# Threshold attention with an RWKV feed-forward: the first five batches taken in two halves of their queries, and new step durations in the planner

## The chip, the cores and the metric

The kernel runs on one core of one Trainium2 chip. The metric is the device time of one launch in microseconds (us); smaller is better. Times are medians of several runs. Besides these there is one profiled execution, whose trace all rows below come from. Engines are named as the profile names them: PE is the matrix engine (its weight loads are PEld), DVE the vector engine, ACT the scalar engine, POOL GpSimd, SP the engine whose queue issues every DMA of this kernel.

## What is computed

Attention of 8 batches, 8 heads, 576 positions and head dimension 64, in which every probability whose score is more than tau under its row's largest is dropped; its output feeds an RWKV channel mix (called FFN here) of width 512 and inner width 1024.

```python
scores = scale * np.matmul(q, k.transpose(0, 1, 3, 2))
thresh = np.max(scores, axis=-1, keepdims=True) - tau
scores = np.where(scores >= thresh, scores, -1000000000.0)
attn = np.exp(scores - np.max(scores, axis=-1, keepdims=True))
attn = attn / (np.sum(attn, axis=-1, keepdims=True) + 1e-09)
x = np.matmul(attn, v)            # then heads side by side: (8, 576, 512)

x_prev = x shifted by one position, zero first
xk = mu_k * x + (1.0 - mu_k) * x_prev
xr = mu_r * x + (1.0 - mu_r) * x_prev
k = np.maximum(xk @ w_k, 0.0)     # 512 -> 1024
v = k * k @ w_v                   # 1024 -> 512
r = 1.0 / (1.0 + np.exp(-(xr @ w_r)))
out = r * v
```

## The kernel before

**The work.** Heads are taken in pairs, four pairs (hp) to a batch. A *job* is one pair of one batch; a *unit* is one block of 128 queries of both heads (kind P, blocks 0 to 3) or the last 64 queries of both heads together (kind T). A P unit makes two score tiles of 128x576, a T unit one; so a batch has 36 score tiles, and the 8 batches have 288. The counter `n` numbers these tiles in the order in which jobs are listed.

**A job's operands** (`operands`): one DMA of queries and keys into `raw` (two buffers), a scaling on ACT (L412), the high part `hi` on ACT (L430, one buffer), the rest `lo` on POOL in two instructions (L436, one buffer), eight DMAs (L455) that stack both into `st1` and `st2` (three buffers each, two of which one job holds), and a DMA of `v` (two buffers). The first two jobs are `plain` and skip `hi`, `lo` and `st`.

**A unit** (`softmax`, `turn_pair`, `turn_last`): scores on PE (L517 from `st` for P units, L492 from `hi` and `lo` directly for T units), row maximum on DVE (L551), threshold and exponential on ACT (L559, L567), mask and sum on DVE (L575), the reciprocal on DVE (L585, L586), the division on POOL (L600), transposes on PE (L624), and their eviction (L642 on ACT, L644 on DVE). With more than `EARLY` tiles behind it, the second of a unit's two big evictions goes to DVE; until then both go to ACT.

**Attention's product** (`attend`, L704) is made for two groups of a job: group 0 from query blocks 0 and 1, group 1 from 2 and 3; the T unit goes with group 0, or with the second part where the job is halved. While its key is under `EARLY` it is cut in five PE steps.

**The FFN** (`ffn_chunk`) works on 256 positions: mixing on POOL, DVE and ACT (L797 to L827), 96 matmuls with w_k (L849), squares on ACT and POOL (L857 to L872), 24 matmuls with w_r (L891), a sigmoid, 48 matmuls with w_v (L913), and the products to the output (L919, DMAs L929). There are 16 chunks from groups and 2 more from the T queries of four batches each, 18 in all. A group's chunk can start when all four pairs of the batch have that group.

**Halving.** Batch 0 is already listed in two parts, which is the only place where the order of units differs:

```python
halved = {0: ([0, 1], [2, "T", 3])}
```

All four pairs run blocks 0 and 1 first, then all four run blocks 2, T and 3. Each part of each pair is a job of its own, so its operands are loaded twice. The other batches run T, 0, 1, 2, 3 of one pair after another.

**What sets the order.** Nothing is scheduled at run time: `Plan.order` places all steps in one list, by expected start on their engine (`s.occ`, `s.lat`, DMA times), then by key. Matmuls and transposes of attention have keys that are 1000 lower than the FFN's, so the FFN fills what they leave on PE. `LATE` puts 0.3 us on attention's PE steps that start after `FROM`; `SOFT` makes the FFN's and the weights' steps on DVE and ACT look later than they are. On the chip each engine runs its own list strictly in order, and so does SP's queue.

**Weights.** 20 pieces of the three weight matrices are taken from 64-bit words by `weight` during the first part of the order: one ACT step, four DVE steps (L355, L369, L376, L386), an ACT and a POOL step each.

Of the kernel before, what the change touches and what calls it, by code (L numbers as in the profile page):

```python
# [48 lines left out]
class Plan:  # L49

    HOP, LATE, FROM = 0.05, 0.3, 150.0
    SOFT = {"DVE": 0.3, "ACT": 0.3}

    def __init__(self):
        self.steps = []
# [54 lines left out]
    def order(self, loose=()):  # L112
# [23 lines left out]
        pipe = 0.0  # L136
# [2 lines left out]

        def when(s):  # L140
            t = s.ready
            more = {}
            for b in s.allocs:
                if id(b) in placed:
                    continue
                m = more.get(b.tag, 0)
                more[b.tag] = m + 1
                if b.tag not in loose and self.tags[b.tag][turn[b.tag] + m] is not b:
                    return None
                h = sorted(freed[id(o)] if o else -1.0 for o in held[b.tag] if not (o and left[id(o)]))  # L150
                if len(h) <= m:
                    return None
                t = max(t, h[m] + self.HOP)
            return t

        total = len(steps)
        while len(out) < total:
            best = None
            for e, cand in open_.items():
                f = free[e]  # L160
                pick = None
                for i in cand:
                    s = steps[i]
                    t = when(s)
                    if t is None:
                        continue
                    t = max(t, f)
# [7 lines left out]
            _, e, i, t = best  # L175
            s = steps[i]
# [2 lines left out]
            free[e] = t + s.occ  # L179
            if e == "DMA":  # L180
                pipe = max(pipe, t) + s.kb / 260.0
                s.end = max(t + 2.2, pipe + 1.5)
            else:
                s.end = t + s.lat
            for b in s.allocs:
                if id(b) not in placed:
                    placed.add(id(b))
                    h = held[b.tag]
# [26 lines left out]
def tile_threshold_attention_then_rwkv_ffn(  # L215
# [12 lines left out]
    V, A, G, PE, SY = nc.vector, nc.scalar, nc.gpsimd, nc.tensor, nc.sync  # L228
# [26 lines left out]
    plan = Plan()  # L255
    add = plan.add
    DQ = 0.55
    W0, W1, W2, W3, AVK = 3.0, 3.5, 50.0, 2.0, 4.5
    PREP, PB, VB, COLD, EARLY = 6, 2, 2, 24, 16
    EV = ("ACT", 0.49), ("DVE", 0.6)  # L260
    KMAX, KEXP, KMASK = 0.0, 0.0, 0.5

# [6 lines left out]
    def fixed(name, shape, dtype=F32):  # L269
# [13 lines left out]
        writes=[(small, 0)],  # L283
        key=-100,
# [5 lines left out]
        reads=[(small, 0)],  # L290
# [32 lines left out]
    def weight(j, name, w, c, f, key, wait):  # L323
# [8 lines left out]
        def t():  # L332
# [18 lines left out]
        )  # L351
        add(
            "DVE",
            0.46,
            lambda: V.tensor_scalar(t(), t(), W_MIN, W_MAX, op0=ALU.max, op1=ALU.min),  # L355
            writes=box,
            key=key,
# [5 lines left out]
        def word(y):  # L363
# [1 line left out]

        add(
            "DVE",
            0.46,
            lambda: V.tensor_scalar(u(), u(), 0x07FFFFFF, 3, op0=ALU.bitwise_and, op1=ALU.logical_shift_left),  # L369
            writes=box,  # L370
            key=key,
        )
        add(
            "DVE",
            0.7,
            lambda: V.scalar_tensor_tensor(  # L376
                u(), word(1), 0xC0000000, u(), op0=ALU.bitwise_and, op1=ALU.bitwise_or
            ),
# [3 lines left out]
        )  # L382
        add(
            "DVE",
            0.7,
            lambda: V.scalar_tensor_tensor(  # L386
                u(), word(0), 29, u(), op0=ALU.logical_shift_right, op1=ALU.bitwise_or
            ),
# [74 lines left out]
    def scores(unit, ss, key):  # L463
# [32 lines left out]
        if unit["kind"] == "T" or job["plain"]:  # L496

            last = unit["kind"] == "T"

            def both():  # L500
                for z in range(2):
                    for h in range(2):
                        hr = slice(h * D, (h + 1) * D)
                        o = ss[1].get()[hr, z, 0:HS] if last else ss[h].get()[:, z, 0:HS]
                        q = slice(SM, S) if last else slice(c * P, (c + 1) * P)
                        PE.matmul(o, raw.get()[hr, q], raw.get()[hr, keys(h, z)], start=True, stop=True)

            occ = 1.2 if last or key > COLD else 2.3
            add("PE", occ, both, reads=[raw], writes=list(ss.values()), key=key - 1000, lat=occ + 0.25)
            return  # L510
        for y in range(2):
# [15 lines left out]
    def softmax(unit):  # L527
# [56 lines left out]
        def invert():  # L584
# [2 lines left out]

        add(
            "DVE",
            0.29,  # L590
            invert,
            reads=[(sm, (2, y)) for y in ys],
            writes=[(sm, (3, y)) for y in ys],
# [24 lines left out]
    def transposes(p, y, at, key, to):  # L618
# [6 lines left out]
                    pt.get()[:, c, :], p.get().rearrange("p y s -> p (y s)")[:, o : o + P], ident.get()  # L625
                )

        occ = 0.109 * len(at)
        add(
            "PE",  # L630
            occ,
# [122 lines left out]
    def ffn_chunk(kind, b0, g, key):  # L754
# [35 lines left out]
        for hc in range(0, NCT, 2):  # L790
# [9 lines left out]
            for j in range(2):  # L800
# [11 lines left out]
                                op1=ALU.add,  # L812
                            )

                add("DVE", 0.8 if nseg == 1 else 1.57, scale, reads=[diff, mu_sb, *sr], writes=[d], key=key)
                add(
                    "ACT",
                    0.52,
# [116 lines left out]
        plan.soft = False  # L935


    halved = {0: ([0, 1], [2, "T", 3])}
    PLAIN = 2
    jobs = []  # L940
    n = 0
# [94 lines left out]
```

## Time and profile before

| | |
|---|---|
| median of 3 runs | 1117.92 us (1116.38 to 1119.11) |
| the profiled execution's own time | 1118.3 us |
| span of the profiled execution, first to last instruction | 1116.5 us |
| mean granted PE clock in it | 0.972 of full speed |
| busy: PE / DVE / ACT / POOL | 93% / 70% / 66% / 52% |

Between the span and the execution's own time lie 1.8 us. Busy shares are means over stages of different kinds: the first batch with the weights, seven batches in which attention and FFN are mixed, and an end in which only FFN chunks are left.

### The profile page before, as it was taken

The page shows a single profiled execution, that of the slowest core. Times are in us where ns is not written, and L with a number is a line of the kernel's source. Part 1 is how long each engine was busy: PE and PEld are TensorE (multiplying, and loading weights), DVE is VectorE, ACT ScalarE, POOL GpSimd, SP SyncE. Part 2 cuts the span into 40 slices and gives each one's busy share as a digit, 9 for nine tenths or more (in the row PEclk, how much of TensorE's full clock was granted, in tenths as well). Part 3 has the DMA queues.
Part 4 walks back from the last instruction along what each step waited for, and adds up shares of the span by engine and source line. Part 5 has one row for each costly group of instructions (what it writes and reads, how often), then busy time and mean ns, then how long its engine had stood idle before and what let it go on. Part 6 is the DMA issues. An engine that isn't in the chain of part 4 may idle for free.

```text
span 1116.5 us, 19374 instructions
## 1 busy us (share of the span) xinstructions
PE 1037.2 (93%) x6832; PEld 852.4 (76%) x6832; DVE 785.5 (70%) x1712; ACT 736.0 (66%) x1543; POOL 578.6 (52%) x582
## 2 busy tenths in 40 slices
PE   5767878898999999999999999999999989999998
PEld 3446656776877878778789878886788869788887
DVE  6889988877878878877887749765888488422220
ACT  5676776675885876776878666775687557344443
POOL 3575765544564555554656535554465544444441
PEclk8777989999999999999999999999999999999999
DMA  6997365544444435444455314441544141000000
GB/s 218 241 269 226 92 162 132 127 113 119 103 102 119 118 84 139 116 110 111 111 130 137 89 43 121 101 108 37 128 115 118 34 92 39 19 20 20 20 19 19
DMA packets 40639, 117.78 MB, mean 105 GB/s; under 512 B 6752, under 2 KB 6752, under 8 KB 40544
## 3 DMA queue, kind: packets, MB, share of 16 engines
q1 hardware_dynamic: 40544, 116.55, 41.0%
q8 instruction: 55, 0.90, 0.3%
q14 instruction: 40, 0.33, 0.1%
HBM read 44.70 MB, written 9.44 MB: 48 GB/s over the span
## 4 chain that ended last, share of the span: by engine, by line
PE 73%; DVE 13%; ACT 6%; DMA 4%; issue 3%; POOL 1%; SPq 0%; POOLq 0%; ACTq 0%
PE w L913 16%; PE w L849 15%; PE w L704 11%; PE w L624 11%; PE s L517 10%; PE w L891 8%; DVE p L575 4%; PE s L492 2%; ACT p L567 2%; DVE sm L551 2%; DMA raw<-in_qk 1%; DVE sm L585 1%; DMA st<-lo 1%; DMA wk<-in_w_k 1%; DVE mk L806 1%
## 5 line engine op out<-in xcount | busy, mean ns | idle before, releaser
L600 POOL TENSOR_SCALAR p<-p,sm 128x576 f32<-128x576 f32 x288 | 225.5, 792 | 268.9 <-DVE sm L586 227.1
L575 DVE SCALAR_TENSOR_TENSOR p<-s,sm,p 128x576 f32<-128x576 f32 x288 | 232.4, 813 | 58.3 <-ACT p L567 57.1
L551 DVE TENSOR_REDUCE sm<-s 128x1 f32<-128x576 f32 x288 | 210.8, 751 | 40.6 <-PE s L517 27.9
L849 PE MATMUL w<-xk,wk 128*128 128x256 f32 x1728 | 231.0, 284 | 0.0
L913 PE MATMUL w<-wv,k 128*128 128x512 f32 x864 | 221.1, 397 | 0.0
L849 PEld LDWEIGHTS w<-xk,wk 128*128 128x128 f32 x1728 | 216.5, 190 | 1.2 <-issue 0.5
L624 PE MATMUL w<-ident,p 128*128 128x128 f32 x1312 | 197.0, 285 | 19.8 <-POOL p L600 14.8
L567 ACT ACTIVATE p<-s,sm 128x576 f32<-128x576 f32 x288 | 210.2, 730 | 0.6
L624 PEld LDWEIGHTS w<-ident,p 128*128 128x128 f32 x1312 | 156.5, 145 | 58.3 <-POOL p L600 32.1
L913 PEld LDWEIGHTS w<-wv,k 128*128 128x128 f32 x864 | 156.4, 189 | 28.7 <-issue 0.8
L642 ACT ACTIVATE pm<-w 128x512 f32<-128x512 f32 x169 | 99.7, 593 | 98.2 <-PE w L624 96.8
L704 PE MATMUL w<-pm,v 128*64 128x256 f32 (+1 forms) x1024 | 148.4, 425 | 5.2 <-DVE pm L644 4.3
L806 DVE SCALAR_TENSOR_TENSOR mk<-m,mu_sb,xT 128x256 f32<-128x256 f32 x128 | 88.6, 732 | 83.5 <-POOL xk L827 83.4
L517 PE MATMUL s<-st 128*128 128x288 f32 x496 | 119.1, 322 | 27.3 <-DVE p L575 11.7
L827 POOL TENSOR_TENSOR xk<-mk,xk 128x512 fp32r<-128x512 f32 x72 | 94.0, 1306 | 92.8 <-ACT xk L819 87.2
L559 ACT ACTIVATE sm<-sm,small 128x1 f32<-128x1 f32 x288 | 83.5, 290 | 83.4 <-DVE sm L551 80.3
L872 POOL TENSOR_TENSOR k<-r,k 128x512 fp32r<-128x512 f32 x72 | 93.8, 1304 | 81.8 <-ACT k L862 81.5
L704 PEld LDWEIGHTS w<-pm,v 128*64 128x64 f32 x1024 | 71.6, 141 | 64.1 <-issue 10.3
L517 PEld LDWEIGHTS s<-st 128*128 128x128 f32 x496 | 79.7, 193 | 51.4 <-issue 29.0
L436 POOL TENSOR_TENSOR lo<-raw,hi 128x576 fp32r<-128x576 f32 x68 | 102.1, 1518 | 31.2 <-ACT hi L430 23.7
L517 PE MATMUL s<-st,st 128*128 128x288 f32 x496 | 110.6, 305 | 0.0
L891 PE MATMUL w<-wr,xk 128*128 128x512 f32 x432 | 109.4, 396 | 0.4 <-ACT pm L642 0.4
(62 smaller groups left out, 1142.9 us busy)
## 6 DMA issues: line engine op xcount, KB each, us to landing
raw<-in_qk SPq DMA_DIRECT2D x36, 608.0 KB, 5.1
st<-hi SPq DMA_DIRECT2D x68, 304.0 KB, 3.2
st<-lo SPq DMA_DIRECT2D x68, 304.0 KB, 4.3
v<-in_v SPq DMA_DIRECT2D x36, 320.0 KB, 4.2
st<-hi SPq DMA_DIRECT2D x68, 144.0 KB, 3.4
st<-lo SPq DMA_DIRECT2D x68, 144.0 KB, 3.9
out<-sg SPq DMA_DIRECT2D x32, 256.0 KB, 2.0
wk<-in_w_k SPq DMA_DIRECT2D x8, 512.0 KB, 7.5
```

Source lines behind the costliest of these rows:

```text
L436: lambda cs=cs: G.tensor_tensor(lo.get()[:, cs], raw.get()[:, cs], hi.get()[:, cs].bitcast(F32), op=ALU.subtract),
L517: PE.matmul(ss[y].get()[:, z, 0:HS], l.get()[:, c * P : (c + 1) * P], r.get()[:, keys(y, z)], start=(j == 0), stop=(j == 1),)
L551: lambda sv=sv, col=col: V.tensor_reduce(col(0), sv(), axis=AX.XY, op=ALU.max, negate=True),
L567: lambda sv=sv, pv=pv, col=col: A.activation(pv(), sv(), AF.Exp, bias=col(0)),
L575: lambda sv=sv, pv=pv, col=col: V.scalar_tensor_tensor(pv(), sv(), col(1), pv(), op0=ALU.is_ge, op1=ALU.mult, accum_out=col(2)),
L600: lambda y=y: G.tensor_scalar(p.get()[:, y], p.get()[:, y], sm.get()[:, 3, y : y + 1], 0.0, op0=ALU.mult, op1=ALU.add),
L624: PE.transpose(pt.get()[:, c, :], p.get().rearrange("p y s -> p (y s)")[:, o : o + P], ident.get())
L704: PE.matmul(o.get()[hs, 0:n], vt.get()[:, c, hs], pt[:, 0:n], start=(c == 0), stop=(c == 4))
L806: V.scalar_tensor_tensor(d.get()[:, y, o : o + n], diff.get()[:, y, o : o + n], mu_sb.get()[:, j, hc + y : hc + y + 1], prv[:, hc + y], op ...
L849: PE.matmul(h.get()[:, f], l, r, start=(ct == 0 and i == 0), stop=(ct == NCT - 1 and i == 2))
L891: PE.matmul(z.get(), l, r, start=(ct == 0 and i == 0), stop=(ct == NCT - 1 and i == 2))
L913: PE.matmul(vps.get(), l, r, start=(ft == 0 and i == 0), stop=(ft == NFT - 1 and i == 2))
```

## The change

Batches 0 to 4 are listed in two parts instead of batch 0 alone. The planner's durations for the weight steps on DVE, for the reciprocal and the mixing, for PE in the first part of the order and for DMAs become longer; `LATE` starts at 100 us instead of 150 and is also put on buffers; `SOFT` is 0.5 on DVE and 0.2 on ACT; `EARLY` is 30 instead of 16. What one instruction computes is the same. After the change lines up to L141 have the same number, lines L142 to L257 stand three lower, and those behind stand four lower (L513 becomes L517).

```diff
-    HOP, LATE, FROM = 0.05, 0.3, 150.0
-    SOFT = {"DVE": 0.3, "ACT": 0.3}
+    HOP, LATE, FROM = 0.05, 0.3, 100.0
+    SOFT = {"DVE": 0.5, "ACT": 0.2}
...
         def when(s):
             t = s.ready
+            hop = self.HOP
+            if s.eng == "PE" and s.key < -500 and t > self.FROM:
+                hop += self.LATE
...
-                t = max(t, h[m] + self.HOP)
+                t = max(t, h[m] + hop)
...
                 pipe = max(pipe, t) + s.kb / 260.0
-                s.end = max(t + 2.2, pipe + 1.5)
+                s.end = max(t + 2.6, pipe + 1.8)
...
+    HALF = 5
     W0, W1, W2, W3, AVK = 3.0, 3.5, 50.0, 2.0, 4.5
-    PREP, PB, VB, COLD, EARLY = 6, 2, 2, 24, 16
+    PREP, PB, VB, COLD, EARLY = 6, 2, 2, 24, 30
...
         add(
             "DVE",
-            0.46,
+            0.55,
             lambda: V.tensor_scalar(t(), t(), W_MIN, W_MAX, op0=ALU.max, op1=ALU.min),
...
         add(
             "DVE",
-            0.7,
+            0.85,
             lambda: V.scalar_tensor_tensor(
...
-            occ = 1.2 if last or key > COLD else 2.3
+            occ = 1.2 if last or key > COLD else 3.0
...
-        occ = 0.109 * len(at)
+        occ = 0.109 * len(at) * (2.3 if key < COLD else 1)
...
-                add("DVE", 0.8 if nseg == 1 else 1.57, scale, reads=[diff, mu_sb, *sr], writes=[d], key=key)
+                add("DVE", 0.9 if nseg == 1 else 1.6, scale, reads=[diff, mu_sb, *sr], writes=[d], key=key)
...
-    halved = {0: ([0, 1], [2, "T", 3])}
+    halved = {j: ([0, 1], [2, "T", 3]) for j in range(HALF)}
```

In the lists of the engines PE has as many instructions as before; DVE has 8 rows fewer, ACT 35 more, POOL 31 more and SP 160 more, 10 for each of 16 added jobs. Three places show what moves.

PE of the kernel before, with the third pair of batch 1 under way (`wr`, `wv` and `k2` are the FFN's, here of the second chunk, group 1 of batch 0; `st` are scores, `pm` attention's products):

```order
L517 MATMUL s_0_2425<-st1_0_2132 128x288 x2
L517 MATMUL s_0_2425<-st1_0_2132,st2_0_2149 128x288 x2
L891 MATMUL w_0_2308<-wr30_0_870,xk_1_1410 128x512 x3
L913 MATMUL w_1_2442<-wv00_0_1076,k2_0_1905 128x512 x3
L704 MATMUL w_3_2450<-pm_1_2393,v_0_1913 64x256 x8
L704 MATMUL w_3_2450<-pl_1_2402,v_0_1913 64x256 x2
L517 MATMUL s_1_2477<-st1_1_2325 128x288 x2
```

PE of the changed kernel with as many units of attention behind it, the second pair of batch 1's second part (`xk` with a new number is the third chunk's):

```order
L917 MATMUL w_1_2356<-wv60_0_1493,k2_0_1928 128x512 x3
L521 MATMUL s_1_2475<-st1_2_2205 128x288 x2
L521 MATMUL s_1_2475<-st1_2_2205,st2_2_2212 128x288 x2
L917 MATMUL w_1_2356<-wv70_0_1504,k2_0_1928 128x512 x3
L628 MATMUL w_2_2487<-ident_66,p_0_2444 128x128 x4
L628 MATMUL w_0_2496<-ident_66,p_0_2444 128x128
L853 MATMUL w_3_2498<-xk_0_2224,wk00_0_167 128x256 x3
L853 MATMUL w_3_2498<-xk_0_2224,wk10_0_196 128x256 x3
L853 MATMUL w_3_2498<-xk_0_2224,wk20_0_246 128x256 x3
```

The third chunk, which now is group 0 of batch 1 itself, starts here behind 33 units; before it started behind 41, in batch 2.

PE of the changed kernel some rows earlier, at the T unit of the first pair in that second part (L496 are its scores, from `hi` and `lo`):

```order
L496 MATMUL s_1_2391<-hi_0_2169,bd_79 128x288 x2
L496 MATMUL s_1_2391<-lo_0_2198,bd_79 128x288 x2
L628 MATMUL w_2_2400<-ident_66,p_1_2352 128x128 x4
L496 MATMUL s_1_2391<-hi_0_2169,bd_79 128x288 x2
L628 MATMUL w_0_2412<-ident_66,p_1_2352 128x128 x4
L628 MATMUL w_3_2419<-ident_66,p_1_2352 128x128
L521 MATMUL s_0_2423<-st1_1_2193 128x288 x2
L521 MATMUL s_0_2423<-st1_1_2193,st2_1_2201 128x288 x2
L917 MATMUL w_1_2356<-wv20_0_974,k2_0_1928 128x512 x3
```

After the last L496 `hi` and `lo` are free for the next job. That job's first scores (L521 on `st1_0_2438`) stand 25 rows behind that L496; between them stand 18 matmuls with w_v, 27 with w_k, 14 transposes and 8 score matmuls. In the kernel before this stands only in batch 0, since elsewhere the T unit comes first in its job.

SP's queue of the changed kernel for that job:

```order
L412 DMA raw_0_2249<-in_qk 128x1216
L933 DMA out_0<-sg_0_2209 128x512
L425 DMA v_0_2395<-in_v 128x640
L459 DMA st1_0_2438<-hi_0_2421 64x1216
L459 DMA st2_0_2446<-hi_0_2421 64x576
L459 DMA st1_1_2455<-hi_0_2421 64x1216
L459 DMA st2_0_2446<-lo_0_2436 64x576
L459 DMA st2_1_2469<-hi_0_2421 64x576
L459 DMA st2_1_2469<-lo_0_2436 64x576
L459 DMA st1_0_2438<-lo_0_2436 64x1216
L459 DMA st1_1_2455<-lo_0_2436 64x1216
```

These ten loads (with `raw` and `v`) and the output between them are what a half job of two or three units puts through the queue; before, a job of five units did.

More of the change, by code (lines that the diff above doesn't have):

```diff
@@ L367, in weight @@
             "DVE",
-            0.46,
+            0.55,
             lambda: V.tensor_scalar(u(), u(), 0x07FFFFFF, 3, op0=ALU.bitwise_and, op1=ALU.logical_shift_left),
@@ L384, in weight @@
             "DVE",
-            0.7,
+            0.85,
             lambda: V.scalar_tensor_tensor(
@@ L589, in softmax @@
             "DVE",
-            0.29,
+            0.33,
             invert,
```

## The prediction

> **What bounds the kernel now.** I read the page first (busy shares and slices), then cut the span at the ends of the batches, then looked at the attention-free end in the chain of waits, then at single waits on PE. Here are the row of PE, and the slices of PE and of the granted clock (28 us each, in tenths):
>
> ```profile
> PE 1037.2 (93%) x6832; PEld 852.4 (76%) x6832; DVE 785.5 (70%) x1712; ACT 736.0 (66%) x1543; POOL 578.6 (52%) x582
> ...
> PE   5767878898999999999999999999999989999998
> ...
> PEclk8777989999999999999999999999999999999999
> ```
>
> PE is full from the ninth slice on; in the first four it is half to three quarters busy at 0.7 to 0.8 of its clock. I cut the span where 36 score tiles more have been reduced (L551); the first row is one batch of these counts, 37 because one tile straddles the cut. Then the same stretches for all engines: length, then busy time and instructions of PE, PEld, DVE, ACT, POOL, granted clock, DMA share, GB/s. The first eight are batches 0 to 7, the ninth is the end.
>
> ```profile
> 162.00:268.00 106.00, 26.59 (x37) 0.98 0.48 118
> ```
>
> ```profile
> 0.00:162.00 162.00, 116.36 (x611) 85.90 (x612) 138.26 (x260) 110.17 (x225) 96.91 (x86) 0.84 0.73 204
> 162.00:268.00 106.00, 98.00 (x662) 77.49 (x661) 86.75 (x192) 72.61 (x163) 54.75 (x59) 0.98 0.48 118
> 268.00:371.00 103.00, 96.70 (x673) 77.86 (x673) 84.50 (x192) 74.59 (x166) 56.76 (x60) 0.97 0.47 113
> 371.00:475.00 104.00, 101.44 (x727) 83.75 (x726) 84.92 (x189) 77.33 (x174) 57.19 (x61) 1.00 0.47 115
> 475.00:580.00 105.00, 103.29 (x698) 83.52 (x698) 82.97 (x192) 77.27 (x168) 56.39 (x58) 1.00 0.47 115
> 580.00:704.00 124.00, 123.22 (x864) 104.15 (x863) 90.23 (x219) 87.95 (x185) 65.97 (x73) 1.00 0.41 102
> 704.00:833.00 129.00, 123.79 (x866) 104.14 (x865) 93.02 (x202) 90.94 (x192) 68.39 (x70) 1.00 0.39 96
> 833.00:956.00 123.00, 118.53 (x814) 97.85 (x814) 91.29 (x194) 82.26 (x174) 61.53 (x63) 1.00 0.29 68
> 956.00:1116.50 160.50, 155.91 (x934) 137.76 (x932) 33.61 (x79) 62.92 (x101) 60.76 (x56) 1.00 0.06 20
> ```
>
> A busy PE is not a PE at its peak, so I price its FFN work by the end of the chain of waits, where one chunk follows another:
>
> ```profile
> 1028.98 11.30 PE w L849 x96
> 1040.28 5.46 PE w L891 x24
> 1045.74 10.89 PE w L913 x48
> ```
>
> A chunk is 27.65 us of PE, 0.1177 us for a matmul with w_k, 0.2275 with w_r, 0.2269 with w_v; 18 chunks are 497.7 us, before and after. The stretches of L849, L891 and L913 alone give their counts; here batch 1 and the end, the others are read alike:
>
> ```profile
> 162.00:268.00 106.00, 14.06 (x96) 12.75 (x96) 0.98 0.48 118
> 956.00:1116.50 160.50, 57.34 (x480) 57.22 (x480) 1.00 0.06 20
> 162.00:268.00 106.00, 6.73 (x24) 4.14 (x24) 0.98 0.48 118
> 956.00:1116.50 160.50, 31.10 (x132) 24.38 (x132) 1.00 0.06 20
> 162.00:268.00 106.00, 15.82 (x60) 10.67 (x60) 0.98 0.48 118
> 956.00:1116.50 160.50, 66.70 (x288) 53.93 (x288) 1.00 0.06 20
> ```
>
> Batch 1 holds 96 x 0.1177 + 24 x 0.2275 + 60 x 0.2269 = 30.4 us of FFN in 106 us, so 75.6 us are left for attention and idle time. I call that the *rest*. For batches 0 to 7: FFN 24.9, 30.4, 31.5, 37.1, 41.3, 62.3, 60.9, 57.3; rest 137.1, 75.6, 71.5, 66.9, 63.7, 61.7, 68.1, 65.7; in the end FFN 151.9 and rest 8.6. All eight batches have the same attention, so the span is 497.7 us plus the rests, and **the change can only win where a rest gets smaller**, however it spreads the FFN. The rest is 62 to 68 where PE has plenty of FFN to fill in with, 72 to 76 where it has little.
>
> **The change part by part, on the span of 1116.5 us.**
>
> *FFN sooner.* Counting FFN matmuls in the new order up to each batch's last transposes and pricing them as above gives for batches 0 to 7: 24.2, 48.5, 55.3, 51.9, 53.9, 47.2, 33.3, 44.4, and 138.9 in the end. So batches 1 to 4 hold about 52 us each instead of 35, as densely as batches 3 to 7 of today. For these I take the mean rest of those five, (66.9 + 63.7 + 61.7 + 68.1 + 65.7) / 5 = 65.2.
>
> *Operands twice.* 16 jobs more, each with these instructions:
>
> ```profile
> L412 ACT ACTIVATE raw<-raw,small 128x576 f32<-128x576 f32 x36 | 27.8, 776 | 6.9 <-DMA raw<-in_qk 6.8
> L430 ACT ACTIVATE hi<-raw 128x1216 fp32r<-128x1216 f32 x34 | 41.5, 1220 | 17.1 <-PE s L492 15.5 <-DMA st<-lo 1.2 <-ACT pl L642 0.5
> L436 POOL TENSOR_TENSOR lo<-raw,hi 128x576 fp32r<-128x576 f32 x68 | 102.1, 1518 | 31.2 <-ACT hi L430 23.7
> raw<-in_qk SPq DMA_DIRECT2D x36, 608.0 KB, 5.1
> st<-lo SPq DMA_DIRECT2D x68, 304.0 KB, 4.3
> v<-in_v SPq DMA_DIRECT2D x36, 320.0 KB, 4.2
> st<-lo SPq DMA_DIRECT2D x68, 144.0 KB, 3.9
> ```
>
> A job costs ACT 0.78 + 1.22 = 2.0 us and POOL 2 x 1.52 = 3.0 us; four more in a batch are 8 and 12 us. With a stretch of about 118 us (65 rest, 52 FFN) ACT goes from 77 to 77 + 8 plus some 7 for the extra half chunk, 92 of 118; POOL from 57 to about 76; DVE from 85 to 88. All have room beside a PE at 95% or more: no cost there. The bytes of a job are 608 + 320 + 4 x (304 + 144) = 2720 KB (each of `hi` and `lo` goes out twice in both sizes); four more turn 115 GB/s into (115 x 105 / 1000 + 10.9) MB in 118 us = 195 GB/s, and the DMA share from 0.47 to 0.47 x 195 / 115 = 0.80. Batch 0 ran 204 GB/s at 0.73, so this fits, with less slack.
>
> *The place that gets tight.* In a second part T is the last but one unit, and `hi` and `lo` are held until its scores are done. The next job's scores then wait for ACT, POOL and SP in a row. In batch 0 of today that was:
>
> ```profile
> 130.86 0.50 PE L492 MATMUL s<-hi,bd 128*128 128x288 f32 x2 [1.06 <-DVE p L575]
> 131.47 0.43 PE L492 MATMUL s<-hi,bd 128*128 128x288 f32 x2
> 131.93 1.22 ACT L430 ACTIVATE hi<-raw 128x1216 fp32r<-128x1216 f32 x1 [0.33 <-PE s L492]
> 133.86 2.94 POOL L436 TENSOR_TENSOR lo<-raw,hi 128x576 fp32r<-128x576 f32 x2
> 137.34 1.86 SPq L455 DMA_DIRECT2D st<-lo  x3
> 142.23 0.50 PE L517 MATMUL s<-st 128*128 128x288 f32 x2 [2.24 <-DVE xT L369]
> 144.63 0.82 PE L517 MATMUL s<-st 128*128 128x288 f32 x2 [1.63 <-DVE p L575]
> 145.80 0.82 PE L492 MATMUL s<-hi,bd 128*128 128x288 f32 x2
> ```
>
> From T's last scores (131.90) to the next job's first (142.23) 10.3 us passed, and PE idled 2.24 and 1.63 us for them and their follower. The row names DVE as releaser, but the last load before it was issued at about 138.0, and with the 3.9 us of such a load it landed at about 142: I read the wait as one for that load. The new order puts between the same two places 18 x 0.2269 + 27 x 0.1177 = 7.3 us of FFN and 14 transposes and 8 scores, some 2.5 us: 9.8 us against 10.3. So a tight boundary should cost about 0.5 us. There are three in each second part and one into the following first part, 15 in batches 1 to 4 (batch 5 begins with T): 7.5 us, 1.9 a batch. Bounds: 0 (the work covers it) and 3.9 us (both waits above). I take 0.5, since the order leaves more FFN there than batch 0 had. If that cover were gone, what is late next is DVE's L551 and the FFN matmuls that stand behind the scores in PE's list.
>
> Batches 1 to 4 thus get 4 x (65.2 + 1.9) = 268.4 of rest against 277.7: **-9.3**.
>
> *The later batches.* Batch 5 loses its surplus of FFN (rest 61.7 to 65.2), batch 6 falls to 33 us of it, between batches 2 and 3 of today (70 against 68.1), batch 7 has 44 (65.2 against 65.7): **+3.5 + 1.9 - 0.5 = +4.9**. The end keeps its 8.6 of rest.
>
> *Batch 0.* Its FFN is the same (24.2 against 24.9) and DVE works 138 of 162 us, of which the first 10 wait for the first scores. `EARLY` takes the 5 evictions that DVE made there for ACT, which has 52 us to spare; each is
>
> ```profile
> L644 DVE COPY pm<-w 128x512 f32<-128x512 f32 x119 | 81.6, 686 | 28.3 <-PE w L624 27.7
> ```
>
> so **-3.4**. The new durations and `SOFT` change no work; they move waits. DVE idles about 14 us behind the first 10, so they could win half of that, 7, or lose as much; I take 0.
>
> Sum: 1116.5 - 9.3 + 4.9 - 3.4 = 1108.7 of span; with the 1.8 us around it 1110.5, and the profiled execution (1118.3) was 0.4 above the median: **1110 us**.
>
> **The rivals.**
>
> *The tight boundaries and the fuller queue cost more than the filling wins (slower).* Place: scores of the job behind T, 15 times. For it: the row at 142.23, and landings that are longer at a high DMA share; SP's queue is in order, and an output whose FFN is late stands ahead of such loads. Against it: batch 0 had the weights' DMAs too, and the second wait was partly DVE's. It decides from 0.5 + 7.8 / 15 = 1.0 us each; at 1.5 us each the sum is 1110 + 15 = **1125**, at the full 3.9 us 1161. Such waits also slow what follows: the T scores at 145.80 took 0.82 us a pair where those at 130.86 took 0.50. The Trainium skill's page "TensorE: Matmul & The Clock Gate" (What's actually happening) says that the PE clock falls to half after an idle window of about 3.4 us and stays there until a busy one; by it the 0.5 us waits cost no clock, and by an estimate from that page (half of such a window) the 3.9 us ones up to another 1.7 us each; the trace's pair of waits with slow scores behind it agrees.
>
> *Batches 1 to 4 get as good as the best of today, and batch 0 wins half of its DVE idle time (much faster).* Rest 63.7 (batch 4) in all four: -22.9; batch 0 -10.4; +4.9: 1118 - 28 = **1090**. For it: the clock of 0.98 and 0.97 in batches 1 and 2 would come back to 1.00. Against it: 63.7 was reached with half the loads.
>
> *No change.* Parts of today's low rests come from stretches in which PE ran 96 w_k matmuls at once with no attention between, and the new order has fewer. With a rest of 69 in batches 1 to 4 (-1.7), +4.9 and -3.4 this is **1118**.
>
> *The change doesn't do what it says*: the list shows that it does (third chunk behind 33 units instead of 41), so only the durations could be without effect, which the forecast already has.
>
> **How the numbers follow.** Forecast 0.46, its own range 1102 to 1116 (boundaries 0 to 0.9, batch 0 -7 to +3); slower 0.20 (1121 to 1140); much faster 0.20 (1082 to 1101); no change 0.14 (1116 to 1120). Within 0.2% is 1115.7 to 1120.2, about what a measurement of this kernel can tell. Faster: 0.44 of the forecast and 0.20, so 0.64; same 0.14; slower 0.22. For 8 in 10 the range leaves out the far halves of the outer rivals: 1095 to 1125.
>
> **What would show it.** Right: in batches 1 to 4 stretches of 115 to 121 us with 192 w_k matmuls each, a DMA share near 0.8, batches 6 and 7 near 103 and 110, an end of about 148; PE idle before L521 behind T under 1 us; granted clock 1.00 from batch 1 on. Wrong: stretches over 125 us in batches 1 to 4, with PE waits before L521 that the landing of `st` ends; a batch 0 longer than 165; or POOL's or ACT's steps of `hi` and `lo` late behind other work.

## The result, and the profile after

The changed kernel takes **1130.69 us** (median of 4 runs, 1128.19 to 1133.02) against 1118.51 us before in the same count: ratio 1.0109, 95% interval 1.0078 to 1.0139. It is slower by 12 us where 8 us less was forecast. Its profiled execution took 1128.19 us, with a span of 1126.0.

Here is the profile of the changed kernel, cut at the same places as before: where 36 score tiles more have been reduced. Columns are length, busy time and instructions of PE, PEld, DVE, ACT and POOL, granted clock, DMA share and GB/s; rows are batches 0 to 7 and the end.

```profile
0.00:163.00 163.00, 113.54 (x604) 84.45 (x605) 138.17 (x256) 111.43 (x225) 96.34 (x87) 0.86 0.75 205
163.00:287.00 124.00, 116.19 (x795) 93.87 (x795) 91.32 (x199) 89.77 (x191) 77.72 (x76) 1.00 0.74 187
287.00:416.00 129.00, 120.97 (x813) 99.97 (x812) 91.38 (x196) 91.65 (x188) 75.81 (x74) 0.99 0.72 179
416.00:541.00 125.00, 118.47 (x797) 96.38 (x796) 92.43 (x196) 89.73 (x189) 73.99 (x72) 0.99 0.74 188
541.00:664.00 123.00, 116.33 (x792) 95.42 (x793) 92.77 (x220) 89.49 (x191) 72.70 (x76) 1.00 0.72 185
664.00:773.00 109.00, 107.32 (x723) 86.80 (x722) 88.77 (x194) 80.15 (x174) 61.37 (x63) 1.00 0.50 123
773.00:872.00 99.00, 98.48 (x729) 82.96 (x728) 82.56 (x190) 76.96 (x172) 56.00 (x60) 1.00 0.49 120
872.00:974.00 102.00, 100.88 (x693) 83.36 (x693) 81.48 (x184) 74.52 (x164) 53.72 (x57) 1.00 0.33 76
974.00:1126.00 152.00, 147.34 (x901) 129.85 (x897) 33.74 (x79) 60.58 (x98) 58.56 (x54) 1.00 0.07 22
```

The work moved as the lists said. Batch 2, from the stretches of its w_k, w_r and w_v matmuls alone, in this order (length, PE busy, PEld busy):

```profile
287.00:416.00 129.00, 28.50 (x192) 25.43 (x192) 0.99 0.72 179
287.00:416.00 129.00, 11.93 (x48) 8.70 (x48) 0.99 0.72 179
287.00:416.00 129.00, 25.92 (x96) 16.88 (x96) 0.99 0.72 179
```

These are 192 x 0.1177 + 48 x 0.2275 + 96 x 0.2269 = 55.3 us of FFN, as counted from the list. But the rest, 129 - 55.3 = 73.7 us, is not 67. By this reading (stretch less FFN at full rate; here with the cuts at the exact tiles):

| rest in us | batch 0 | 1 | 2 | 3 | 4 | 5 | 6 | 7 | end | sum |
|---|---|---|---|---|---|---|---|---|---|---|
| before | 137.3 | 75.1 | 72.2 | 66.5 | 64.0 | 61.7 | 67.9 | 65.5 | 8.6 | 618.8 |
| forecast | 133.7 | 67.1 | 67.1 | 67.1 | 67.1 | 65.2 | 70 | 65.2 | 8.6 | 611 |
| after | 139.6 | 74.1 | 74.3 | 72.7 | 70.8 | 64.4 | 61.8 | 58.9 | 11.5 | 628.1 |

Batches 1 to 4 lost 14 us where they should have won 9, batches 5 to 7 won 10 where they should have lost 5, batch 0 and the end lost 5. These rests come from one profiled execution of each kernel.

What came into the path is told by the chain of waits, shares of the span by engine. First the kernel before, then the changed one with its second row by line:

```profile
PE 73%; DVE 13%; ACT 6%; DMA 4%; issue 3%; POOL 1%; SPq 0%; POOLq 0%; ACTq 0%
```

```profile
PE 59%; DMA 13%; DVE 12%; ACT 6%; POOL 4%; SPq 3%; issue 3%; POOLq 0%; ACTq 0%
PE w L917 13%; PE w L853 12%; PE w L708 10%; PE s L521 9%; PE w L628 8%; DMA st<-lo 7%; PE w L895 6%; DMA st<-hi 3%; SPq L459 3%; DVE p L579 3%; DVE mk L810 3%; DVE sm L555 2%; PE s L496 2%; POOL lo L440 2%; ACT p L571 1%
```

DMAs and SP's queue went from 4% to 16% of the chain, most of it the copies into `st`. In order of time, the chain of the changed kernel at the start of batch 1 is little else (start, length, what):

```profile
169.07 1.01 SPq L459
170.12 6.28 DMA st<-lo
176.71 1.43 POOL lo L440
178.85 1.27 SPq L459
180.81 4.49 DMA st<-hi
185.53 1.22 ACT hi L434
...
191.59 1.57 POOL lo L440
193.19 4.27 DMA st<-lo
...
205.56 5.03 DMA st<-lo
210.63 0.80 PE s L521 x4
```

The matmul at its end is the first score of batch 1's second part, in front of which no T unit stands. PE waited 1.09 us for a copy to land (start, length, instruction, idle time before it):

```profile
210.63 0.54 PE L521 MATMUL s<-st 128*128 128x288 f32 x2 [1.09 <-DMA st<-lo]
```

And this is a boundary behind T late in batch 4. T's scores ended at 637.67. ACT waited for them before it could write `hi` again, and the next job's first scores stand at 648.90:

```profile
637.71 1.22 ACT L434 ACTIVATE hi<-raw 128x1216 fp32r<-128x1216 f32 x1 [1.95 <-PE s L496]
643.81 0.53 PE L521 MATMUL s<-st 128*128 128x288 f32 x2 [1.80 <-DVE p L579]
648.90 0.43 PE L521 MATMUL s<-st 128*128 128x288 f32 x2
```

The wait of 1.80 us is not one for the next job's copies. Counted from the start of the list, that matmul belongs to the second head of block 3 of T's own job, and the semaphore that let it go is DVE's, 0.04 us ahead of it. A copy for the next job landed 0.08 us ahead as well, by chance. The next job's own first scores began without idle time.

To compare runs I add up, for score matmuls from `st`, by how much each began later than the usual spacing behind the matmul ahead of it, where that is over 0.2 us, and ask whether a copy into `st` landed less than 0.3 us ahead. In batches 1 to 4 these *landing waits* are 0.3 us (one) before and 19.5 us (27) after; score waits with another end are 12.5 and 9.5. This is nearness, not cause, and counts too many: the wait of 1.80 us above is among the 27. By the semaphores the profile puts none of PE's score waits down to a landing of `st` before, and 9.4 us in 13 waits after. It does the same for ACT's step of `hi` and POOL's steps of `lo`, which wait until copies out of these buffers have landed. Here are these waits in batches 1 to 4, before and after (total in us, number, longest):

```profile
ACT hi L430 <- DMA st<-lo: 1.2, 3, 0.5
POOL lo L436 <- DMA st<-lo: 0.7, 1, 0.7
```

```profile
ACT hi L434 <- DMA st<-hi: 12.7, 12, 2.3
POOL lo L440 <- DMA st<-lo: 9.6, 4, 3.0
PE s L521 <- DMA st<-lo: 9.4, 13, 1.5
```

### The profile page after: what moved, and what is told of

Same layout as the page of the kernel before. It is cut to its first block, busy times and chain, and to the rows that moved or that the text cites. A ratio compares the mean times of both kernels' runs of the same rounds, so it can differ in the third digit from the quotient of the medians.

```text
span 1126.0 us, 19747 instructions
## 1 busy us (share of the span) xinstructions
PE 1039.5 (92%) x6832; PEld 853.1 (76%) x6832; DVE 792.6 (70%) x1707; ACT 764.3 (68%) x1582; POOL 626.2 (56%) x614
## 4 chain that ended last, share of the span: by engine, by line
PE 59%; DMA 13%; DVE 12%; ACT 6%; POOL 4%; SPq 3%; issue 3%; POOLq 0%; ACTq 0%
PE w L917 13%; PE w L853 12%; PE w L708 10%; PE s L521 9%; PE w L628 8%; DMA st<-lo 7%; PE w L895 6%; DMA st<-hi 3%; SPq L459 3%; DVE p L579 3%; DVE mk L810 3%; DVE sm L555 2%; PE s L496 2%; POOL lo L440 2%; ACT p L571 1%
## 5 line engine op out<-in xcount | busy, mean ns | idle before, releaser
L579 DVE SCALAR_TENSOR_TENSOR p<-s,sm,p 128x576 f32<-128x576 f32 x288 | 233.5, 814 | 92.5 <-ACT p L571 91.4
L853 PE MATMUL w<-xk,wk 128*128 128x256 f32 x1728 | 239.0, 286 | 2.5 <-ACT pm L646 2.2
L917 PE MATMUL w<-wv,k 128*128 128x512 f32 x864 | 223.4, 400 | 0.4 <-ACT pm L646 0.4
L853 PEld LDWEIGHTS w<-xk,wk 128*128 128x128 f32 x1728 | 219.7, 190 | 5.0 <-ACT pm L646 2.6
L628 PE MATMUL w<-ident,p 128*128 128x128 f32 x1312 | 200.9, 286 | 22.2 <-POOL p L604 18.6
L628 PEld LDWEIGHTS w<-ident,p 128*128 128x128 f32 x1312 | 158.9, 146 | 56.2 <-POOL p L604 32.3
L440 POOL TENSOR_TENSOR lo<-raw,hi 128x576 fp32r<-128x576 f32 x100 | 151.5, 1531 | 74.2 <-ACT hi L434 34.2
L521 PE MATMUL s<-st 128*128 128x288 f32 x496 | 120.2, 324 | 39.7 <-DVE p L579 27.9
L708 PE MATMUL w<-pm,v 128*64 128x320 f32 (+1 forms) x1024 | 142.4, 418 | 0.8 <-DVE pm L648 0.8
L831 POOL TENSOR_TENSOR xk<-mk,xk 128x512 fp32r<-128x512 f32 x72 | 93.1, 1293 | 89.0 <-ACT xk L823 82.9
L810 DVE SCALAR_TENSOR_TENSOR mk<-m,mu_sb,xT 128x256 f32<-128x256 f32 x128 | 98.3, 808 | 61.5 <-POOL xk L831 60.4
L646 ACT ACTIVATE pm<-w 128x512 f32<-128x512 f32 x174 | 102.7, 592 | 42.5 <-PE w L628 41.6
L521 PEld LDWEIGHTS s<-st 128*128 128x128 f32 x496 | 78.8, 191 | 68.4 <-issue 37.6
L648 DVE COPY pm<-w 128x512 f32<-128x512 f32 x114 | 78.4, 688 | 52.4 <-PE w L628 52.0
```

What stands on the lines that cost most here:

```text
L440: lambda cs=cs: G.tensor_tensor(lo.get()[:, cs], raw.get()[:, cs], hi.get()[:, cs].bitcast(F32), op=ALU.subtract),
L521: PE.matmul(ss[y].get()[:, z, 0:HS], l.get()[:, c * P : (c + 1) * P], r.get()[:, keys(y, z)], start=(j == 0), stop=(j == 1),)
L579: lambda sv=sv, pv=pv, col=col: V.scalar_tensor_tensor(pv(), sv(), col(1), pv(), op0=ALU.is_ge, op1=ALU.mult, accum_out=col(2)),
L628: PE.transpose(pt.get()[:, c, :], p.get().rearrange("p y s -> p (y s)")[:, o : o + P], ident.get())
L708: PE.matmul(o.get()[hs, 0:n], vt.get()[:, c, hs], pt[:, 0:n], start=(c == 0), stop=(c == 4))
L810: V.scalar_tensor_tensor(d.get()[:, y, o : o + n], diff.get()[:, y, o : o + n], mu_sb.get()[:, j, hc + y : hc + y + 1], prv[:, hc + y], op ...
```

## The experiments

All of them compute the same outputs. Ratios are against runs of the kernel before on the same chip, with 95% intervals. Line numbers in rows are those of each kernel. Every edit lets the planner place all steps anew, so the rest of a batch also moves where its own work is as it was; sums of rests come from one profiled execution each.

### The parts apart: numbers alone, halves alone

```diff
-    HALF = 5
+    HALF = 1
```

> The changed kernel with batch 0 alone in halves: only the planner's numbers are changed. Theory A (the wait for hi, lo and their copies behind the T unit of a second part costs the time): no added place of that kind, so no slower than before, 1112 to 1120 us. Theory B (the added loads fill the DMAs and SP's queue): the same 1112 to 1120. Theory C (the new step durations put steps in worse places): 1126 to 1134, like the changed kernel.

Measured: 1106.2 us, ratio **0.9896** (0.9867 to 0.9926). The new numbers alone make the kernel *faster* by 1%, which no theory had. Landing waits are 1.0 us, and the profile puts no wait of PE, `hi` or `lo` in batches 1 to 4 down to a landing of `st`. The batches 0 to 4 of this run:

```profile
0.00:157.00 157.00, 113.06 (x601) 83.78 (x602) 135.93 (x256) 110.56 (x228) 94.64 (x85) 0.85 0.76 211
157.00:250.50 93.50, 86.71 (x619) 69.09 (x618) 80.91 (x189) 69.32 (x162) 54.30 (x59) 0.98 0.52 127
250.50:353.00 102.50, 101.26 (x691) 82.19 (x690) 84.61 (x191) 75.10 (x165) 55.72 (x58) 1.00 0.47 116
353.00:452.00 99.00, 98.07 (x717) 81.85 (x716) 80.04 (x186) 73.89 (x166) 52.99 (x57) 1.00 0.50 123
452.00:563.50 111.50, 109.80 (x745) 89.11 (x745) 87.21 (x196) 80.98 (x177) 59.92 (x63) 1.00 0.44 108
```

Batches 2 to 4 have rests of 62.1, 62.5 and 64.8 with 40.6, 36.7 and 46.3 us of FFN, batch 1 still 74.6 with 18.8.

The other way round, `halved` over five batches in the kernel before, with the old numbers:

```diff
-    halved = {0: ([0, 1], [2, "T", 3])}
+    halved = {j: ([0, 1], [2, "T", 3]) for j in range(5)}
```

> The kernel before with batches 0 to 4 in halves and all the planner's numbers as they were. Theories A and B: 1126 to 1140 us, as slow as the change or slower, since the plan then counts on shorter DMAs. Theory C: 1108 to 1118.

Measured: 1157.3 us, ratio **1.0326** (1.0283 to 1.037), landing waits 34.5 us: slower than any theory's range. So the change is two changes of opposite sign. On top of the new numbers the halves cost 1.0109 / 0.9896 = 1.0215, some 24 us; on top of the old ones 36.

### T first, and smaller loads

```diff
-    halved = {j: ([0, 1], [2, "T", 3]) for j in range(HALF)}
+    halved = {j: ([0, 1], ["T", 2, 3]) for j in range(HALF)}
```

> The changed kernel with the T unit first in each second part (T, 2, 3 instead of 2, T, 3); loads and work are the same. Theory A: hi and lo are free two units earlier, the waits before L521 that the landing of st ends fall from 9 us to under 4 us in batches 1 to 4, time 1112 to 1120 us. Theory B: 1126 to 1134, since bytes and issues are the same.

Measured: 1130.74 us, ratio 1.0098 (1.006 to 1.0135). The landing waits fell from 19.5 to 5.4 us as theory A said (PE's by the semaphores from 9.4 to 3.1), and the time did not follow. In the same batches ACT's waits for a landing before `hi` rose from 12.7 to 20.2 us, the sum of the first and fourth row here, and POOL's stayed:

```profile
ACT hi L434 <- DMA st<-hi: 11.3, 11, 2.0
POOL lo L440 <- DMA st<-lo: 9.5, 7, 2.7
PE s L521 <- DMA st<-lo: 3.1, 5, 1.6
ACT hi L434 <- DMA st<-lo: 8.9, 6, 3.0
```

The rest of batches 1 to 4 fell only from 291.9 to 284.9, that of 5 to 7 rose from 185.1 to 192.4.

The smaller loads, of which the host's order and the sizes are shown here:

```diff
-        add("DMA", DQ, lambda: SY.dma_start(raw.get(), qk[b, hp]), writes=[raw], key=key - PREP - 5, kb=576)
+        if part is None:
+            a, e, q0, q1, kt = 0, W, 0, S, S
+        elif part == 0:
+            a, e, kt = S - CH, W, 0
+            q1 = e - a
+            q0 = q1 - CH
+        else:
+            a, e, q0, q1, kt = 0, W - CH, 0, S - CH, S - CH
+        n = e - a
+        add("DMA", DQ, lambda: SY.dma_start(raw.get()[:, 0:n], qk[b, hp][:, a:e]), writes=[raw], key=key - PREP - 5, kb=n // 2)
...
+    for b_ in range(HALVED):
+        x = qk[b_]
+        qk[b_] = np.concatenate([x[..., 256:s], x[..., s:], x[..., :256]], axis=-1)
```

> The changed kernel where a half job loads and splits only the queries that it uses (896 or 960 of 1216 columns; the host orders the columns of batches 0 to 4 so that each part is one piece). Issues are the same, bytes of a halved pair fall by a quarter. Theory B: the DMA share in batches 1 to 4 falls from 0.73 to about 0.55 and the time to 1112 to 1120 us. Theory A: the chain behind T gets some 1.5 us shorter but stays, 1118 to 1126.

Measured: 1127.68 us, ratio 1.0082 (1.0055 to 1.0109). The DMA share fell to 0.60, 0.58 and 0.57 in batches 2 to 4 and the landing waits to 13.9 us, but the time moved by 3 us, outside both theories' ranges. The rest of its batch 0 is 16 us smaller (124.0), and batch 1 gave that back (92.5). Both edits together:

> Both remedies at once: T first in the second parts and only the used queries loaded. So far T first took the score waits behind a landing in batches 1 to 4 from 19.5 to 5.4 us and the smaller loads took them to 13.9, but the times stayed at 1131 and 1128. Theory A2 (what the halves cost is these waits, and the single runs hide it by their spread): 1108 to 1118 us. Theory D (the earlier FFN chunks cost the time by taking DVE, ACT and POOL ahead of the softmax): 1124 to 1132, the waits only change their name.

Measured: 1116.76 us, ratio 0.9967 (0.9948 to 0.9985), landing waits 3.1 us. Together they take some 15 us off the changed kernel, so theory A2 holds for that much. It is still 8 us (by the ratios) to 11 us (by the times) above the numbers alone.

### The loads without the early FFN

In batches 1 to 4 the two parts of one pair follow each other, so there are the same 16 added jobs, but no chunk comes much before the end of its batch:

```diff
-        for part, order in enumerate(halved.get(b, (["T", 0, 1, 2, 3],))):
-            for hp in range(NPAIR):
+        parts = list(enumerate(halved.get(b, (["T", 0, 1, 2, 3],))))
+        turns = [(part, order, hp) for part, order in parts for hp in range(NPAIR)]
+        if b > 0:
+            turns.sort(key=lambda x: x[2])
+        for part, order, hp in turns:
```

> The changed kernel, but in batches 1 to 4 the two parts of a pair follow each other (0, 1 then 2, T, 3 of one pair, then the next pair): 16 added jobs with all their loads as in the change, while FFN chunks come at the end of a batch as they did before. Theory A2 or B (added loads and the waits for them): 1124 to 1135 us. Theory D (chunks that come earlier): 1104 to 1112, like the step durations without halves.

Measured: 1147.46 us, ratio **1.0235** (1.0203 to 1.0266). It is slower than either theory's range, and theory D falls: without the earlier chunks the time is 1.0235 - 1.0109 longer, some 14 us, and the 16 added jobs with their loads, splits and T's place cost 1.0235 / 0.9896, some 38 us. Not all of the 14 us need be the chunks, since the order of jobs differs too. The difference lies in batch 1 alone, the first row here (rest 96.0 against 74.1 in the changed kernel); in batches 2 to 4 the rest is 218.8 against 217.8.

```profile
157.00:287.50 130.50, 109.93 (x682) 86.50 (x681) 88.46 (x193) 81.90 (x175) 68.72 (x68) 0.91 0.72 177
287.50:410.70 123.20, 118.49 (x800) 95.58 (x799) 89.24 (x200) 92.06 (x192) 77.66 (x76) 1.00 0.76 193
```

Two halved batches instead of five:

```diff
-    HALF = 5
+    HALF = 2
```

> The changed kernel with batches 0 and 1 in halves. Any theory in which each halved batch costs the same: a quarter of the way from 1106 to 1131, 1110 to 1115 us. If early FFN helps where today PE has too little of it (batch 1, rest 75 us in every run so far): 1098 to 1105.

Measured: 1112.21 us, ratio 0.9932 (0.9907 to 0.9957): a sixth (by the ratios) to a quarter (by the times) of the way from one to five, with an interval that overlaps that of one. Batch 1's rest is 78.3 with 47.8 us of FFN, so its early FFN didn't pay even there.

### Which of the new numbers

`HALF = 1` with the new step and DMA durations, but these as before:

```diff
-    HOP, LATE, FROM = 0.05, 0.3, 100.0
-    SOFT = {"DVE": 0.5, "ACT": 0.2}
+    HOP, LATE, FROM = 0.05, 0.3, 150.0
+    SOFT = {"DVE": 0.3, "ACT": 0.3}
...
-    PREP, PB, VB, COLD, EARLY = 6, 2, 2, 24, 30
+    PREP, PB, VB, COLD, EARLY = 6, 2, 2, 24, 16
...
-                hop += self.LATE
+                hop += 0.0
```

> Batch 0 alone in halves, and of the planner's numbers only the step and DMA durations new; SOFT, EARLY, FROM and the LATE on buffers as before. If the durations make the gain of 1.0%: 1103 to 1110 us. If SOFT, EARLY and FROM make it: 1114 to 1121.

Measured: 1112.65 us, ratio 0.9924 (0.9901 to 0.9947): the durations make 0.76% of the 1.04%. The rest goes to the other four together; the intervals with and without them overlap, so how much is theirs stays open. Batch 0 has a rest of 133.1 us here, with the old `EARLY`.

### What in an added job costs

Each of these starts from the numbers alone (1106.2 us, one half) and doubles one thing in the unhalved batches 1 to 4. The split into `hi` and `lo`:

```diff
-        add("ACT", 1.1, lambda: A.activation(hi.get(), raw.get(), AF.Copy), reads=[raw], writes=[hi], key=key - PREP)
-        for y in range(2):
+        for _ in range(2 if 1 <= b <= 4 else 1):
+            add("ACT", 1.1, lambda: A.activation(hi.get(), raw.get(), AF.Copy), reads=[raw], writes=[hi], key=key - PREP)
+            for y in range(2):
...
```

> Batch 0 alone in halves with the new planner's numbers (1106 us), and in batches 1 to 4 the split into hi and lo made twice over the same data: 16 times 1.2 us more on ACT and 3.0 us on POOL, which is what 16 added jobs put there, but no added job, copy or DMA. If ACT's and POOL's work is what an added job costs: 1120 to 1132 us. If it is the handing over of operands (buffers, copies, their landing): 1104 to 1111.

Measured: 1111.91 us, ratio 0.9936 (0.991 to 0.9961), 0.4% or some 4 to 6 us more, with an interval that overlaps that of the numbers alone (0.9867 to 0.9926): between the two ranges of the expectation and nearer to the lower one.

The eight copies into `st`:

```diff
                 (t2, up, lo, S, (lo, 0)),
-            ):
+            ) * (2 if 1 <= b <= 4 else 1):
```

> The same 1106 us kernel with the eight copies into st issued twice in batches 1 to 4: 16 times 1.8 MB and 8 issues more on SP, no added job and nothing on ACT and POOL. If the bytes and the issues cost the time: 1118 to 1132 us. If the handing over at an added job start costs it, beside which copies are hidden: 1105 to 1112.

Measured: 1127.42 us, ratio **1.008** (1.0053 to 1.0107), 21 us more, with landing waits of 10.9 us and batches 2 to 4 at a DMA share like the changed kernel's, without any added job there:

```profile
270.00:384.00 114.00, 106.92 (x753) 90.40 (x753) 87.83 (x196) 80.24 (x178) 62.76 (x64) 0.97 0.75 174
384.00:492.50 108.50, 102.88 (x693) 82.14 (x692) 81.83 (x192) 77.56 (x169) 55.96 (x59) 0.98 0.76 177
492.50:603.00 110.50, 105.72 (x746) 87.89 (x746) 83.48 (x193) 77.00 (x171) 56.15 (x60) 0.98 0.71 165
```

The rests there are 72.3, 70.0 and 69.8 instead of 62.1, 62.5 and 64.8. One reserve: the second copy waits in SP's queue until the first has landed, 31.7 us in all by the queue's waits, so part of this price is that the operands are ready later. By the semaphores POOL's steps of `lo` wait 22.5 us for landings in batches 1 to 4, PE 7.0.

The same bytes in twice as many issues:

```diff
-                fn = (lambda dst=dst, rows=rows, src=src, n=n, sl=sl: SY.dma_start(
-                    dst.get()[rows, 0:n].bitcast(F32), src.get()[sl, 0:n].bitcast(F32)
-                ))
-                add("DMA", DQ, fn, reads=[r], writes=[(dst, rows.start)], key=key - PREP, kb=n // 4)
+                cut = [0, n // 2, n] if 1 <= b <= 4 else [0, n]
+                for i, (x0, x1) in enumerate(zip(cut, cut[1:])):
+                    fn = (lambda dst=dst, rows=rows, src=src, x0=x0, x1=x1, sl=sl: SY.dma_start(
+                        dst.get()[rows, x0:x1].bitcast(F32), src.get()[sl, x0:x1].bitcast(F32)
+                    ))
+                    add("DMA", DQ, fn, reads=[r], writes=[(dst, (rows.start, i))], key=key - PREP, kb=(x1 - x0) // 4)
```

> Batch 0 alone in halves with the new planner's numbers (1106 us), and in batches 1 to 4 each copy into st cut in two of half the columns: 128 issues more on SP, the same bytes. If it is SP's queue (its issues, some 0.6 us each, in order) that makes the copies cost time: 1116 to 1128 us, as with the copies issued twice (1127). If it is the bytes: 1104 to 1110.

Measured: 1107.04 us, ratio 0.9876 (0.985 to 0.9901): no difference. The added issues on SP cost nothing that this run shows; the smaller copies also landed sooner (median 2.4 us in batches 2 to 4 instead of 3.4), which could hide a small price. The sum of the rests of batches 2 to 4 is 196.9 here and 189.4 in the numbers alone, at the same time, so differences of this size in that sum say nothing. And the changed kernel with the copies of `hi` issued by ACT:

```diff
-                fn = (lambda dst=dst, rows=rows, src=src, n=n, sl=sl: SY.dma_start(
+                act = src is hi and 1 <= b <= 4
+                fn = (lambda dst=dst, rows=rows, src=src, n=n, sl=sl, act=act: (A if act else SY).dma_start(
...
-                add("DMA", DQ, fn, reads=[r], writes=[(dst, rows.start)], key=key - PREP, kb=n // 4)
+                if act:
+                    add("ACT", 0.06, fn, reads=[r], writes=[(dst, rows.start)], key=key - PREP, lat=4.0)
+                else:
+                    add("DMA", DQ, fn, reads=[r], writes=[(dst, rows.start)], key=key - PREP, kb=n // 4)
```

> The changed kernel (1131 us) with the four copies of hi in batches 1 to 4 issued from ACT's queue instead of SP's: bytes and jobs are the same, SP has 4 issues of 10 less in a job. If SP's queue costs the time: 1112 to 1122 us. If the bytes do: 1126 to 1134, or slower if ACT's own time for an issue hurts the softmax.

Measured: 1207.09 us (three executions at 1204.75 to 1208.21, a fourth at 2085.35, which no run explains), ratio 1.0752 (1.0718 to 1.0787). Bytes are the same, and ACT now pays for its issues between the steps of the softmax. Its own row (minimum, median, maximum in ns), and the wait of PE's weight loads that is longest in all (total in us, number, longest):

```profile
L460 ACTq DMA_DIRECT2D st<-hi x128: 468/608/2266, 144.1 to 695.5; - x128
```

```profile
PEld s L525 <- issue: 94.5, 66, 5.8
```

128 issues at 0.61 us are 78 us on an engine that the softmax waits for. This run doesn't tell bytes from queue, since it added a cost of its own. The Trainium skill's page "DMA: Bandwidth & Descriptors" (Issuing engines are not separate DMA queues) says that issuing from a second engine saves only the sequencer's time. Here there was none to save: twice as many issues on SP left the time as it was (1107.0 against 1106.2 us).

### Versions beyond both

The smaller loads with batch 0 alone in halves, without and with T first:

> Batch 0 alone in halves, new planner's numbers, half jobs load only the queries they use. In the runs with small loads in five batches batch 0 took 141 us instead of 157 to 163, but batch 1 had a rest of 88 to 92 us. If the loss in batch 1 came with its own halves: 1088 to 1100 us. If batch 0's gain is only put off to batch 1: 1103 to 1109.

> The same with T first in batch 0's second part. If the wait behind T matters in batch 0 too: 2 to 6 us under the run with 2, T, 3. Else the same within 2 us.

Measured: 1108.08 us, ratio 0.9907 (0.9873 to 0.9941), and 1105.86 us, ratio 0.9881 (0.9853 to 0.9909). Against the numbers alone batch 0's rest is smaller (124.6 and 127.6 against 134.2) and batch 1's larger (89.5 and 82.9 against 74.6), with batch 1 unhalved too: the gain is only put off, the second answer of the first expectation. Neither can be told from the numbers alone, which are faster than both the kernel before and the changed one.

## Why the prediction was wrong

**Step "Operands twice ... no cost there" failed, and it is the one that turned the sign.** I compared busy times with the length of a stretch and found room on every engine and on the DMAs. The copies alone cost 21 us in unhalved batches (one reserve above) and the split some 4 to 6, which the intervals hardly tell from nothing; the 16 jobs with everything cost 38, and the order with the early chunks gave 14 back. The sums themselves were near: ACT 92 and POOL 76 a batch forecast, 90 and 74 measured; a DMA share of 0.80 forecast, 0.72 to 0.74 measured. Room was not the measure. What counts is when a copy lands: PE can't take work that stands behind the next job's scores in its list, and ACT and POOL can't write `hi` and `lo` again, one buffer each, while copies still read them. Landing of the copies into `st` in batches 2 to 4, minimum, median and maximum in us, before, after, and with the smaller loads in five halved batches:

```profile
DMA to landing us min/median/max: 2.5/3.4/5.2
```

```profile
DMA to landing us min/median/max: 2.3/4.2/10.5
```

```profile
DMA to landing us min/median/max: 2.0/3.1/6.4
```

A load for which every engine had room still made the job's start later.

**Step "The place that gets tight" had the right kind of wait at the wrong place.** I priced 15 boundaries behind T at 0.5 us each, 7.5 us. Of the 13 score waits of PE that the profile ends by a landing, three stand there (1.7 us). Ten (7.7 us) stand where no T is ahead, in front of jobs of a first part or the first job of a second part, like the one at 210.63 above. There the job ahead has only two units, and the chain at the start of batch 1 shows what they hand over: copies land, `lo` and `hi` are written again, the next copies go out. I had no term for that reuse. Waits that the profile ends by a landing of `st`, batches 1 to 4, in us:

| run | PE, scores | ACT, `hi` | POOL, `lo` | sum | ratio of times |
|---|---|---|---|---|---|
| before | 0 | 1.2 | 0.7 | 1.9 | 1 |
| numbers alone | 0 | 0 | 0 | 0 | 0.9896 |
| change | 9.4 | 12.7 | 9.6 | 31.7 | 1.0109 |
| T first | 3.1 | 20.2 | 9.5 | 32.8 | 1.0098 |
| small loads | 7.3 | 5.1 | 20.7 | 33.1 | 1.0082 |
| both | 1.9 | 8.0 | 4.4 | 14.3 | 0.9967 |
| pairs split | 6.0 | 9.3 | 27.2 | 42.5 | 1.0235 |
| copies twice | 7.0 | 7.4 | 22.5 | 36.9 | 1.0080 |
| split twice | 0 | 2.5 | 0 | 2.5 | 0.9936 |
| issues twice | 0 | 1.1 | 0 | 1.1 | 0.9876 |
| two halved | 7.1 | 4.0 | 4.7 | 15.8 | 0.9932 |
| halves alone | 10.8 | 12.0 | 10.7 | 33.5 | 1.0326 |

T first and the smaller loads each moved these waits to another engine and left the sum, and the time hardly moved; both edits together halved the sum and took some 15 us off. That these waits are the price is my reading of runs side by side; the halves alone, on the old numbers, are slower than their sum would say. A second buffer for `hi` and `lo`, which would test it, was not tried. In batches 2 to 4 the rests add up to 217.8 in the change, 208.9 with T first, 205.4 with small loads, 199.3 with both, 189.4 without halves. The last 10 us of this stay open: a plan with the same time as the numbers alone has 196.9. The slower rival named the boundaries behind T and the fuller queue, at 1125 us with a chance of 0.20, and the time lies in its range of 1121 to 1140. Its longer landings hold; its place does not, and more issues on SP alone cost nothing.

**Step "FFN sooner" took too much from one profile.** I read from the first five full batches that the rest is small where PE has FFN to fill in with, and gave batches 1 to 4 a rest of 65.2 (67.1 with the boundaries). They have 49 to 55 us of FFN, as forecast, and rests of 74.1, 74.3, 72.7 and 70.8: with half jobs more FFN didn't bring the rest down. In the numbers alone batch 3 has the FFN that it had before (36.7 against 37.1 us) and a rest of 62.5 instead of 66.5, so part of the large rests came from the plan. Batch 2 has 10 us less rest with 9 us more FFN, and batch 1 has 74.6 as against 75.1 with 11 us less FFN, so the premise itself is neither confirmed nor refuted. Why the later batches came out at -10 instead of +4.9 is open too. Their rest is 185.1 with 125 us of FFN in the change, 182.7 with 123 in the split pairs and 194.2 with 183 in the numbers alone, but about 199 with 130 in the halves alone.

**Step "Batch 0": the term for the durations was the largest of all, and I set it to 0.** I argued that durations change no work, only waits, and looked for these in batch 0 alone. In the run with the numbers alone batch 0 won 3.1 us. That this is near my 3.4 for `EARLY` is luck: with the old `EARLY` and the new durations batch 0 won 4.2. Batches 1 to 4 won 13.8 (277.8 to 264.0). In the change itself batch 0 lost 2.3.

**What was right:** the FFN's place (192 w_k matmuls in each of batches 1 to 4, 140 us left in the end against 138.9), the stretches of batches 1 and 4 within a few us of the 115 to 121 named as right (124, 123), the granted clock of 0.99 to 1.00 from batch 1 on, and the sign by which to tell: stretches of 123 to 129 us with waits that a landing of `st` ends.

## What to carry to other kernels

Work that is loaded twice to make other work ready sooner isn't free because each engine has room for it. Price the time from its issue to its landing at the new traffic, and ask what stands behind the first instruction that needs it in a list that runs in order, and which buffer is not free before it lands.

A change of two parts wants two predictions: here new numbers in the planner, most of all longer durations, won 1%, and the reordering that came with them lost 2%.

A correlation between stages of one profile (small rest where there is much FFN) is no mechanism: with twice the loads, half as much FFN again left the rest where it was or made it larger. And an event close ahead of the end of a wait need not be what ended it; ask which semaphore the instruction waits for, and of which job it is.

## What was not expected of the hardware

Copies of 64 rows inside the chip's memory landed after much the same time at twice the size: 3.2 us for 304 KB and 3.4 for 144 KB before (medians of the copies of `hi`). Cut in two, 152 KB took 2.5 and 72 KB 2.3 us, and twice as many issues left the time as it was, so more and smaller copies are at least no worse here. With the traffic the time grew: in batches 2 to 4 the median of all these copies was 3.4 us at a DMA share of 0.47 and 4.2 us at 0.72 to 0.74.

An issue of a DMA took its engine about 0.6 us also on ACT (median 608 ns, 468 to 2266), where SP took 588 for the same copies in the changed kernel. On SP 128 more issues cost nothing that the runs show; moved to ACT, 128 of them made the kernel some 72 us (by the ratios) to 76 us (by the times) slower, near the 78 us that they take together.
